# A fused attention and mixture-of-experts kernel: another written-out order for attention, and pass one starting its seven-product form one unit earlier

## The chip, the cores and the metric

One core of a Trainium2 chip runs the whole program in a single launch. The metric is the device time of that launch in microseconds (us). TensorE is called PE here, VectorE DVE, ScalarE ACT, GpSimd POOL, and SP is the queue that issues most DMAs.

## The reference, cut to what matters

```python
# attention: 4 batches x 8 heads, 576 tokens, 64 wide
scores = scale * q @ k.T + (cum[:, None] - cum[None, :])      # cum = cumsum(log f), causal
attn = softmax(scores);  x = (attn @ v) as 2304 tokens x 512
# mixture of experts: 8 experts, 512 -> 1024 -> 512
logits = x @ w_gate;  P = exp(logits - max)
for _ in range(8):                                            # alternate row and column scaling
    P /= P.sum(1) + 1e-9;  P /= P.sum(0) + 1e-9;  P *= N / E
out = sum over e of P[:, e] * (relu(x @ w1[e]) @ w2[e])
```

Everything is fp32. The kernel keeps it so by splitting each operand of a product into a high and a low part (fp32r) and issuing three matmuls: high by high, high by low, low by high.

## The kernel before, in words

**Attention** works on 16 pairs of heads (`attend`, L405). Each pair is cut into some 85 steps, each bound to one engine or to a choice of two. The steps aren't scheduled when the kernel is built: the string `ORDER` lists their numbers, and each engine gets its steps in the order in which they stand there. A letter behind a number picks the engine where a step has a choice (a for ACT, d for DVE, p for POOL). The order also decides which buffer a step gets, since buffers are handed out along the list. The last two steps of a pair write its part of x: the high part (`x_hi_part`, on ACT or DVE) and the low part (`x_lo_part`, L842, on POOL alone). The weight products of the first two blocks of 256 hidden features of expert 0, on the first 768 tokens, are steps too (`early`, lines 904 and 924) and stand between attention's.

**Pass one** takes the remaining 30 blocks (a unit: one expert, 256 of its hidden features) over the same 768 tokens. The loop runs from L1384; unit m computes the hidden features (first half), and the second half of unit m-1 (`second`, line 924: 36 matmuls of 512 columns) follows it. The first half has two forms. `first_plain` (48 matmuls of 384 columns) multiplies x by w1 as they are. `first_fast` (42 matmuls, line 1292) is a seven-product scheme on 2 x 2 blocks. It needs three kinds of prepared operands:

- sums of x: `token_sums` (L1188) forms four sums T1 to T4 for each of two slices c of the contraction, eight additions on POOL each; `part_sums` (L1212) splits them, high on ACT, low by four subtractions on POOL. They are made once for the pass.
- sums of w1: `weight_sums` (L1237) forms S1 to S4, four additions on POOL, for each unit.
- their split: `split_sums` (L1247) rounds on ACT (line 1251 writes all four high sums at once) and subtracts on POOL (line 1255: the four low sums, S1 first; lines 1253 and 1259: low parts of the plain blocks A11, A12, A22). S1 to S4 are kept in the buffer `early_w["w1"]`, which the plain form uses for w1 itself.

```python
    for m, (n, e, fb, segs) in enumerate(work):
        fast, fast_next = m >= PLAIN, m + 1 >= PLAIN
        ...
        if m < KH:
            sums = token_sums(0, m)
            for t in sums:
                pass
```

With `PLAIN = 3` the units 0, 1 and 2 are plain and unit 3 is the first fast one; the sums of x for c = 0 and c = 1 are formed during units 0 and 1. `first_fast` issues its products in the order A11·B11, S2·T2, S1·T1, S3·T3, A12·B21, S4·B22, A22·T4. The tile framework orders pass one by its own estimate, except for instructions pinned by `keep_in_program_order`; what it settles on is fixed when the program is built, and every engine runs its queue in that order. Each fast unit's prepared w1 is also written to DRAM (`keep_w1`). Between the products run the gate's 8 scaling rounds (`gate_weights`, L1133), a few small instructions at each `go_on()`, which the plain form calls four times per unit and `second` six times.

**Passes two and three** (line 1736 and 1838) run the rest of the tokens in the seven-product form on both halves, ordered by a list scheduler (`arrange`). Units whose w1 wasn't kept in pass one are prepared there by `prepare_w1`.

Of the kernel before, what the change touches and what calls it, by code (L numbers as in the profile page):

```python
# [146 lines left out]
def pool_two(n): return 0.02 + n / 410  # L147
# [14 lines left out]
5 4 7 0 9 8 6 10 20 1 3 98 2 21a 95 22d 102 23 17 24 103d 104a 181 11 25a 26d 128 14 93 28 12a 27 349 13a 99 33 94  # L162
15d 29a 34 42 16a 92 30 36 31d 100a 32 56 97 101a 35 43 47 37 44 180 51 57 41 48 61 19 52 58 96 112 45 39 62 445 53
108 40 54 267 113a 63 125 59 114a 269 38 55 126 64 71 183 60 124 110d 75 357 49 73 72a 127 109d 356 50 123 115 116
76a 186 121 79 111 122 81 119a 184 74a 80d 129 139 65 120 182 117d 130 118 185 46 140 82a 83 18 131 141 135 77 187 66
84a 144 268 137 67p 78a 133 85 142 138 149 147 134 68 86a 150 151 69a 70d 199 191 152 148 361 87 200d 202d 153 360
203 201 193d 264 143 145 263 132 204 192d 210 146 194 208 136 195 211 105 89 165 206 88 106 196a 173 159 205 90d 197a
107 166a 169 154 91 171 266 160a 174d 198 167 170a 265 161 163 172a 162d 207 222 1059 164a 168d 1056 212 213 223 227
225 224 209 214 175 226 218 270 216 215 230 219 228 217 1060 220 229 1061 232 1057 234 233 231 246 1058 1062 274 235
189 244 247d 275a 242 188 155p 245a 276d 278 277 243a 190 1068 279d 280a 236 614 289 252 281 615 156 295 221 253d 359  # L170
282 1074 158a 237 362 283a 157a 285d 287 284 256 254 1065 286 290 257a 176 248 534 255a 294 177 296 532 249a 178d 288
291 305 238a 533 301 179 310 297 358 302 306 315 298 444 313 307 293 250 1075 316 292 314 299 363 308 1069 251a 303
317 309 239 318 304 375 311 319 258 448 241d 312 447 240d 446 376d 300 377 378d 379 320 367 272 260 321 332 259 273
368a 383 330 369d 322a 371 271 370 382 331a 336 333d 323 384 372a 340 385 373d 530 1066 328 374 386 342 337a 531 334
387 329d 341a 457 442 388 335d 338 343a 443 458a 625 459d 339a 461 324 460 389 1067 464a 326 261a 626d 344 325 1063
628 380 462d 327 465 381 463 390 262 708 396 528 392 397 394 797 627a 1064 398 393 449 395 403 345 366 391 399 408
365 401 400 1076 346 402 410 406 453 347a 404 350 706 407 348 409 364 455a 454a 547 411 1113 429 550a 1070 618 412
551 351d 469 456 620 1071 405 548d 470 619 549 435 543 467 1072 436d 354 466 425 430a 544d 472 431 352 433 355 474
413 432a 427 617 546 426a 414 494 616 415a 434a 496 471 416 495 421 473 428a 707 497 489 468 1073 529 498 475 535 492
422a 1080 490 493 420 476 1077 491 353 478 480 417 423 477 482 484 418 479 545d 481 419 629 485 424a 539 487 794 486  # L180
633 630d 437 712 541a 631a 488 636d 710 634d 632 483 560 711 635 1078 637 499 793 1079 792 556 521 552 439 509 709
553 522a 517 510a 798 557 511 518a 515 555 512d 451 513 516a 558 507 438 450 514a 554 500 540d 519 452 508a 559 1081
542 501a 520a 502 561 621 575 568 564 570 569 566 580 565 562 578 567 504 1086 571 506 579 1087 573 503 582 563 576
717 505 574 523 581 879 572 1088 878 577 639 583 643 718d 584 642 720 645 440a 656 638 537 524 719a 640 525 593 1110
644 657 536 526a 607 721 641 659 595 658 881 646 1083 594d 722a 796 608d 1084 723a 724 596a 538 441 601 585 713 597
1085 602a 599 598a 603 1082 527 586 600a 647 604a 661 587a 650 588 648 651 605 652 649 664 668 653 666 606d 660 1089
665 667 609 669 654 670 736 589 662 732 591 655 734 663 590 730 731 592 748 671 737 795 689 738 749 624 672 1092 751
750 623 1090 673d 733 690a 687 674 1091 735 685 688a 691 611 799 686a 725 610 683 880 692a 739 612d 622 728a 726a 613
729 684a 753 727 678 740 742 811 746 676 743 1098 744 741 677 1099 754 747 1093 675 1094 814a 756 812a 681 884 889
815 682a 813 882 807 890a 679 820 883 808a 892 693 816 803 680a 817 891d 970 758 809d 821 694a 804d 805a 969 760 755  # L190
823 806 695 1337 819 759 752 967 761 818 757 810 966 824 762 964 965 745 834 822 697 716 696 783 714 835 771 885 784a
763 785 773 786a 775 772a 774d 764 777 776a 837 825 765d 838 698d 766 839 830 778a 699 715 826 700 831 832 968 827
828 840 1336 833 893 829 842 781 1167 841 779 1095 895d 1166 782d 843 846 701d 844 902 767 780a 1100 907 845 836 1101
768 903 979 847 1114 906 769 897 908 983 980d 787 900a 770 909 898a 986a 982 848 704 905 702 981d 901 910 894a 1253
899 987 1111 849 1340 896 1168 1115 850 863 789 788 1170 851a 869 984a 864a 985 1169 861 1112 1102 871 859 870a 790d
# [1891 lines left out]
```

## Time and profile before

| | |
|---|---|
| time, median of 3 runs | 1630.55 us (1630.13 to 1631.98) |
| the profiled execution | 1630.41 us, of which the span of its instructions 1628.6 us |
| PE busy | 1619.9 us, 99% of the span |
| DVE, POOL, ACT busy | 1310.4, 1122.2, 767.3 us |
| attention with the early products | the first 211.6 us |
| pass one | from there to about 690 us |

Matmuls are pipelined: a row of the timeline gives the start of its first matmul and a length up to the modelled end of its last, which overlaps the next row. So the price of a matmul is read from start to start of consecutive rows, or from a count in a stretch, not from the length of one. A bracket at the end of a row is the time its engine idled before it and what ended that.

### The profile page before, as it was taken

How to read it: one execution, taken by the hardware profiler on the slowest of the kernel's cores; microseconds unless marked ns; L12 is line 12 of the kernel's file. 1: busy time of each engine (PE TensorE's matmuls, PEld its weight loads, DVE VectorE, ACT ScalarE, POOL GpSimd, SP SyncE). 2: the span in 40 equal slices, each digit the busy share in tenths (PEclk: the TensorE clock that was granted, in tenths of full speed). 3: DMA queues.
4: the chain of work that ended last, by engine and by line, in shares of the span. 5: the costliest groups of instructions: out<-in, count | busy, mean ns of one | idle time of the engine just before them, and what ended most of it. 6: DMA issues, size and time to landing. Idle time of an engine off the chain costs nothing.

```text
span 1628.6 us, 29751 instructions
## 1 busy us (share of the span) xinstructions
PE 1619.9 (99%) x9641; PEld 1534.1 (94%) x9641; DVE 1310.4 (80%) x2742; ACT 767.3 (47%) x1918; POOL 1122.2 (69%) x1431
## 2 busy tenths in 40 slices
PE   8999999999999999999999999999999999999999
PEld 7888889989899899899999999999999999999998
DVE  8888778776676776788898888878988888788887
ACT  8887743443333333344454444444444444344443
POOL 6556385777788887778777767666666666566675
PEclk9999999999999999999999999999999999999999
DMA  6666325655566656576777776657665555565552
GB/s 154 157 159 160 92 64 175 185 178 185 181 197 184 193 185 209 181 233 192 229 222 220 221 224 201 187 175 218 197 198 162 171 178 170 164 173 171 168 167 70
DMA packets 257025, 291.24 MB, mean 179 GB/s; under 512 B 76291, under 2 KB 168686, under 8 KB 256870
## 3 DMA queue, kind: packets, MB, share of 16 engines
q1 hardware_dynamic: 256438, 288.94, 59.5%
q8 instruction: 77, 1.26, 0.3%
q14 instruction: 78, 0.64, 0.1%
q10 hardware_dynamic: 432, 0.39, 0.1%
HBM read 222.43 MB, written 66.83 MB: 178 GB/s over the span
## 4 chain that ended last, share of the span: by engine, by line
PE 98%; ACT 0%; POOL 0%; DVE 0%; DMA 0%; issue 0%; SPq 0%
PE bankA L1838 28%; PE bankA L1736 20%; PE po L924 16%; PE ph L1292 12%; PE bankM L1736 9%; PE pv L823 3%; PE ph L904 2%; PE pt L775 2%; PE ps L614 2%; PE pq L496 1%; PE ps L660 1%; PE bankA L1889 1%; PE pt L779 0%; PE ps L607 0%; PE bankA L1922 0%; PE pg L858 0%
## 5 line engine op out<-in xcount | busy, mean ns | idle before, releaser
L1847 DVE TENSOR_TENSOR sum<-bankA,sum 128x384 f32<-128x384 f32 x406 | 224.3, 553 | 52.9 <-PE bankA L1838 51.4
L1736 PE MATMUL bankA<-t,wn 128*128 128x384 f32 x1314 | 248.3, 334 | 0.0
L924 PE MATMUL po<-early_w,hh 128*128 128x512 f32 x768 | 239.1, 392 | 0.0
L1736 PEld LDWEIGHTS bankA<-t,wn 128*128 128x128 f32 x1314 | 229.4, 188 | 0.0
L924 PEld LDWEIGHTS po<-early_w,hh 128*128 128x128 f32 x768 | 142.4, 188 | 28.7 <-issue 0.7
L1666 POOL TENSOR_TENSOR fourw<-w 128x256 f32<-128x256 f32 x124 | 91.7, 740 | 92.2 <-DMA w<-in_moe_w_dram 92.2
L924 PE MATMUL po<-early_w,hl 128*128 128x512 f32 x384 | 150.3, 391 | 0.0
L1298 DVE TENSOR_TENSOR u<-ph,u 128x384 f32<-128x384 f32 x189 | 101.9, 552 | 56.8 <-PE ph L1292 53.2
L1337 DVE SCALAR_TENSOR_TENSOR acc<-po,prob,acc 128x512 f32<-128x512 f32 x144 | 106.6, 747 | 50.5 <-PE po L924 48.8
L1838 PE MATMUL bankA<-xhi,early_w 128*128 128x384 f32 x576 | 128.3, 334 | 0.0
L1255 POOL TENSOR_TENSOR early_w<-ws,early_w 128x256 fp32r<-128x256 f32 x108 | 93.9, 898 | 39.7 <-ACT early_w L1251 38.5
L1736 PE MATMUL bankM<-xhi,wn 128*128 128x384 f32 x424 | 119.0, 334 | 0.0
L1232 ACT CAST early_w<-w 128x512 fp32r<-128x512 f32 x66 | 41.0, 622 | 161.1 <-issue 137.9
L1838 PE MATMUL bankA<-xlo,early_w 128*128 128x384 f32 x522 | 116.8, 335 | 0.0
L1529 POOL TENSOR_TENSOR w2n<-fourw,w2n 128x256 fp32r<-128x256 f32 x105 | 79.6, 761 | 43.2 <-PE bankA L1838 21.5
L1838 PE MATMUL bankA<-xhi,w2n 128*128 128x384 f32 x480 | 108.9, 334 | 0.0
L1233 POOL TENSOR_TENSOR early_w<-w,early_w 128x512 fp32r<-128x512 f32 x56 | 71.9, 1305 | 44.8 <-ACT early_w L1232 44.8
L1838 PEld LDWEIGHTS bankA<-xhi,early_w 128*128 128x128 f32 x576 | 102.4, 188 | 0.0
L1838 PE MATMUL bankA<-xlo,w2n 128*128 128x384 f32 x438 | 99.4, 334 | 0.0
L910 ACT ACTIVATE hh<-u 128x384 fp32r<-128x384 f32 x108 | 56.1, 522 | 91.4 <-DVE u L1298 91.3
L1529 POOL TENSOR_TENSOR early_w<-w,early_w 128x256 fp32r<-128x256 f32 x96 | 72.4, 760 | 37.7 <-ACT early_w L1524 37.7
L1529 POOL TENSOR_TENSOR early_w<-fourw,early_w 128x256 fp32r<-128x256 f32 x117 | 89.5, 772 | 12.0 <-ACT early_w L1524 11.3
(332 smaller groups left out, 4518.6 us busy)
## 6 DMA issues: line engine op xcount, KB each, us to landing
wn<-w1d SPq DMA_DIRECT2D x440, 256.0 KB
w<-in_moe_w_dram SPq DMA_DIRECT2D x266, 256.0 KB
w1d<-early_w SPq DMA_DIRECT2D x54, 512.0 KB
w1d<-wa SPq DMA_DIRECT2D x54, 384.0 KB
w1d<-four SPq DMA_DIRECT2D x70, 128.0 KB
dn<-cum_d SPq DMA_DIRECT2D x14, 576.0 KB
pb<-p_d SPq DMA_DIRECT2D x16, 384.0 KB
q<-in_q_dram SPq DMA_DIRECT2D x32, 128.0 KB
```

Source lines behind the costliest of these rows:

```text
L910: nc.scalar.activation(out=hh[:, 0:w], in_=ph[:, 0:w], func=AF.Relu)
L924: nc.tensor.matmul(po[:, cols], ht[:, ts], wt[:, ft, cols], start=(ft == 0 and n == 0), stop=(ft == FB - 1 and n == 2))
L1233: a = lo_on.tensor_tensor(out=lo[:, s], in0=r, in1=hi[:, s].bitcast(F32), op=ALU.subtract)
L1255: nc.gpsimd.tensor_tensor(out=wsum[1][:, n], in0=t[:, n], in1=wsum[0][:, n].bitcast(F32), op=ALU.subtract)
L1292: nc.tensor.matmul(ps, ws[y][:, c], xs[z], start=(c == 0 and m == 0), stop=(c == KH - 1 and m == 2))
L1298: nc.vector.tensor_tensor(out=out, in0=in0, in1=in1, op=ALU.add)
L1337: a = nc.vector.scalar_tensor_tensor(out=to, in0=po, scalar=prob[:, t, e:e + 1], in1=to, op0=ALU.mult, op1=ALU.add)
L1529: eng(e).tensor_tensor(out=dst(1), in0=src(), in1=dst(0).bitcast(F32), op=ALU.subtract)
L1666: eng(en).tensor_tensor(out=vs[o](), in0=a(), in1=b(), op=op)
L1736: nc.tensor.matmul(ps, wt[:, y, c * P:(c + 1) * P], x[z], start=(start and c == 0 and m == 0), stop=(c == KH - 1 and m == 2), skip_group_c ...
L1838: nc.tensor.matmul(at_(b)[:, 0:HT], at_(w)[y][:, k * P:(k + 1) * P], at_(h)[:, z], start=(i == 0), stop=(i == 5))
L1847: nc.vector.tensor_tensor(out=to, in0=at_(b)[:, 0:HT], in1=to, op=ALU.add)
```

## The change

- `ORDER` is replaced throughout. The steps are the same but for the choices of engine: 47 go from ACT to DVE, 46 from DVE to ACT, and the last step of the last pair, its low part of x, goes to DVE.
- `x_lo_part` may run on DVE for the last four pairs (it does for the last one only).
- `PLAIN` is 2: unit 2 is now the first fast unit, and its prepared w1 is kept.
- The sums of x for c = 0 are formed on DVE. Those for c = 1 stay on POOL. All are formed and split in unit 0, c = 1 after c = 0.

```diff
 ORDER = """
-5 4 7 0 9 8 6 10 20 1 3 98 2 21a 95 22d 102 23 17 24 103d 104a 181 11 25a 26d 128 14 93 28 12a 27 349 13a 99 33 94
+0 1 5 4 20 6 7 22a 9 10 2 21a 23 24 25a 26d 102 104a 103d 126 11 12a 33 34 27 8 28 29a 31d 32 30 13a 99 100a 101a 14
...
-        z = step(i + 0.73, {"POOL": pool_two(S)}, x_lo_part, after=[a], uses=[xf])
+        lo_on = {"POOL": pool_two(S), "DVE": dve_sbuf(S)} if i >= NPAIR - NP else {"POOL": pool_two(S)}
+        z = step(i + 0.73, lo_on, x_lo_part, after=[a], uses=[xf])
...
-    def token_sums(g, c):
+    def token_sums(g, c, on=nc.gpsimd):
...
         def pinned(**kw):
-            tc.keep_in_program_order(nc.gpsimd.tensor_tensor(**kw))
+            a = on.tensor_tensor(**kw)
+            if on is nc.gpsimd:
+                tc.keep_in_program_order(a)
...
-    PLAIN = 3
+    PLAIN = 2
...
-        if m < KH:
-            sums = token_sums(0, m)
+        if m == 0:
+            sums = token_sums(0, m, nc.vector)
             for t in sums:
                 pass
...
-        if m < KH:
-            part_sums(0, m, t)
+        if m == 0:
+            part_sums(0, 0, t)
+            for t in token_sums(0, 1):
+                pass
+            part_sums(0, 1, t)
```

The program's matmuls go from 9305 to 9299: 48 of the plain form less, 42 of the fast form more. Line numbers behind L842 are one to six higher in the changed kernel.

Three places show what moved. The first is the start of PE's queue, in attention; `pq` are the turned q and k of the first pair, `pc` the spread decay (from `cumparts`), `ps` the first scores. Before:

```order
L337 MATMUL warm<-ones 128x128 x8
L496 MATMUL pq<-ident,q 128x128 x4
L389 MATMUL pc<-cumparts,pick 128x288 x2
L496 MATMUL pq<-ident,k 128x128 x4
L389 MATMUL pc<-cumparts,pick 128x288 x4
```

And now:

```order
L337 MATMUL warm<-ones 128x128 x8
L496 MATMUL pq<-ident,q 128x128 x4
L496 MATMUL pq<-ident,k 128x128 x4
L389 MATMUL pc<-cumparts,pick 128x288 x4
L537 MATMUL pq<-ident,rz_105 128x128
```

The turning of k stands ahead of the spread of the decay, no longer behind its first half. Over the whole of attention PE changes its kind of work 206 times before and 194 times now, by the same count on both orders.

The second place is POOL's queue from the end of attention to the first fast unit. `early_w_110` is the low part of w1 or of its sums, `ts` the sums of x, `t_4214` and `t_4237` their low parts for c = 0 and c = 1, `ws` the sums of w1, `wa_4236` the low parts of A11, A12 and A22. Before:

```order
L330 TENSOR_TENSOR xlo<-xf,xhi 128x576 x5
L1233 TENSOR_TENSOR early_w_110<-w,early_w_109 128x512 x2
L1197 TENSOR_TENSOR ts<-xhi,xlo 128x384 x2
...
L1197 TENSOR_TENSOR ts<-ts,xlo 128x384
L1220 TENSOR_TENSOR t_4214<-ts,t_4214 128x384 x4
L1197 TENSOR_TENSOR ts<-xhi,xlo 128x384 x2
...
L1197 TENSOR_TENSOR ts<-ts,xlo 128x384
L1220 TENSOR_TENSOR t_4237<-ts,t_4237 128x384 x4
L1241 TENSOR_TENSOR ws<-w 128x256
...
L1255 TENSOR_TENSOR early_w_110<-ws,early_w_109 128x256 x4
```

And now:

```order
L1236 TENSOR_TENSOR early_w_110<-w,early_w_109 128x512 x2
L1223 TENSOR_TENSOR t_4214<-ts,t_4214 128x384 x4
L1198 TENSOR_TENSOR ts<-xhi,xlo 128x384 x2
L1198 TENSOR_TENSOR ts<-ts,xhi 128x384
L1256 TENSOR_TENSOR wa_4236<-w,wa_4235 128x256
...
L1262 TENSOR_TENSOR wa_4236<-w,wa_4235 128x256
L1198 TENSOR_TENSOR ts<-xhi,ts 128x384
L1198 TENSOR_TENSOR ts<-ts,xlo 128x384
L1223 TENSOR_TENSOR t_4237<-ts,t_4237 128x384 x4
L1244 TENSOR_TENSOR ws<-w 128x256
...
L1258 TENSOR_TENSOR early_w_110<-ws,early_w_109 128x256 x4
```

The eight sums for c = 0 are gone from POOL; the rest of the chain keeps its order, with the three low parts of A11, A12 and A22 moved in among the sums for c = 1. In the elided parts stand the other sums, one instruction each.

The third place is PE's queue where the second half of unit 0 ends and the first half of unit 2 begins. Before:

```order
L924 MATMUL po<-early_w_112,hh_4244 128x512
L924 MATMUL po<-early_w_111,hl_4245 128x512
L904 MATMUL ph<-xhi,early_w_109 128x384
L904 MATMUL ph<-xlo,early_w_109 128x384
L904 MATMUL ph<-xhi,early_w_110 128x384
```

And now:

```order
L925 MATMUL po<-early_w_112,hh_4244 128x512
L925 MATMUL po<-early_w_111,hl_4245 128x512
L1295 MATMUL ph<-xhi,wa_4235 128x384
L1295 MATMUL ph<-xlo,wa_4235 128x384
L1295 MATMUL ph<-xhi,wa_4236 128x384
...
L1295 MATMUL ph<-t_4214,early_w_109 128x384 x2
L1295 MATMUL ph<-t_4214,early_w_110 128x384
```

Six matmuls of A11·B11 come first; the next product, S2·T2, reads the high sums of w1 (`early_w_109`) and at its third matmul the low ones (`early_w_110`).

## Rows read from the trace of the kernel before

**Rows 1.** The page, part 1 (busy time and instructions) and part 4 (the chain).

```profile
PE 1619.9 (99%) x9641; PEld 1534.1 (94%) x9641; DVE 1310.4 (80%) x2742; ACT 767.3 (47%) x1918; POOL 1122.2 (69%) x1431
...
PE 98%; ACT 0%; POOL 0%; DVE 0%; DMA 0%; issue 0%; SPq 0%
```

**Rows 2.** Busy us by stretch: PE, PEld, DVE, ACT, POOL, clock, DMA share, GB/s.

```profile
0.00:211.58 211.58, 207.50 (x1812) 168.85 (x1813) 167.39 (x590) 166.66 (x527) 111.06 (x198) 1.00 0.54 139
...
900.00:1000.00 100.00, 100.00 (x579) 100.00 (x578) 87.55 (x178) 48.07 (x123) 72.97 (x95) 1.00 0.72 215
```

**Rows 3.** Who PE waited for: us in total, times, longest.

```profile
PE pc L389 <- DVE cumparts L1032: 1.6, 1, 1.6
```

**Rows 4.** PE's timeline at the start: start, length, engine, line, count.

```profile
1.05 3.62 PE L337 MATMUL warm<-ones 128*128 128x128 f32 x16 [1.05 <-DVE ones L334]
4.66 0.63 PE L496 MATMUL pq<-ident,q 128*128 128x128 f32 x4
```

**Rows 5.** PE's timeline where attention ends and unit 0 begins.

```profile
208.69 0.74 PE L924 MATMUL po<-early_w,hh 128*128 128x512 f32 x2
209.27 0.40 PE L924 MATMUL po<-early_w,hl 128*128 128x512 f32 x1
...
211.75 0.34 PE L904 MATMUL ph<-xlo,early_w 128*128 128x384 f32 x1
212.25 0.61 PE L904 MATMUL ph<-xhi,early_w 128*128 128x384 f32 x2 [0.16 <-POOL early_w L1233]
...
213.24 0.34 PE L904 MATMUL ph<-xlo,early_w 128*128 128x384 f32 x1
213.95 0.62 PE L904 MATMUL ph<-xhi,early_w 128*128 128x384 f32 x2 [0.37 <-POOL early_w L1233]
```

**Rows 6.** PE's timeline: last of unit 0's first half, its second half, unit 2.

```profile
220.82 0.34 PE L904 MATMUL ph<-xhi,early_w 128*128 128x384 f32 x1
...
230.85 0.63 PE L924 MATMUL po<-early_w,hh 128*128 128x512 f32 x2
...
239.32 0.33 PE L904 MATMUL ph<-xhi,early_w 128*128 128x384 f32 x1
```

**Rows 7.** ACT's timeline: first split of x's sums, and the sums of w1.

```profile
221.97 0.82 ACT L1217 CAST t<-ts 128x768 fp32r<-128x768 f32 x1
...
247.96 1.05 ACT L1251 CAST early_w<-ws 128x1024 fp32r<-128x1024 f32 x1 [1.46 <-PE ph L904]
```

**Rows 8.** POOL's timeline from the first split of x's sums to w1's low sums.

```profile
222.89 4.37 POOL L1220 TENSOR_TENSOR t<-ts,t 128x384 fp32r<-128x384 f32 x4
227.34 2.05 POOL L1197 TENSOR_TENSOR ts<-xhi,xlo 128x384 f32<-128x384 f32 x2
...
236.45 4.09 POOL L1220 TENSOR_TENSOR t<-ts,t 128x384 fp32r<-128x384 f32 x4
...
249.09 2.82 POOL L1255 TENSOR_TENSOR early_w<-ws,early_w 128x256 fp32r<-128x256 f32 x4 [2.46 <-ACT early_w L1251]
```

**Rows 9.** Two of POOL's lines over the run: count, ns least, median, most.

```profile
L1197 POOL TENSOR_TENSOR ts<-ts x8: 1008/1020/1481, 218.3 to 598.4; 128x384 f32<-128x384 f32 x8
L1255 POOL TENSOR_TENSOR early_w<-ws,early_w x108: 727/790/1165, 249.1 to 656.9; 128x256 fp32r<-128x256 f32 x108
```

**Rows 10.** DVE's timeline: operands from SBUF, 512 columns, beside a busy and an idle POOL.

```profile
230.53 2.91 DVE L1233 TENSOR_TENSOR early_w<-w,early_w 128x512 fp32r<-128x512 f32 x2 [0.48 <-ACT early_w L1232]
...
256.53 0.69 DVE L1233 TENSOR_TENSOR early_w<-w,early_w 128x512 fp32r<-128x512 f32 x1
```

**Rows 11.** Timelines of PE and of DVE at the gate's last round.

```profile
315.25 0.28 PE L1171 MATMUL pc<-cs,ones 128*128 128x8 f32 x2
317.32 0.60 PE L1182 MATMUL pt<-ident,prob 128*8 128x128 f32 x4
...
313.32 1.04 DVE L913 SCALAR_TENSOR_TENSOR hl<-u,hh 128x384 fp32r<-128x384 f32 x1
316.69 0.31 DVE L1175 TENSOR_TENSOR prob<-prob,ca 128x144 f32<-128x144 f32 x1
```

**Rows 12.** Busy us by stretch, behind PE's last matmul.

```profile
1624.65:1628.50 3.85, 0.00 (x0) 0.00 (x0) 0.48 (x2) 0.16 (x1) 0.00 (x0) 1.00 0.62 204
```

More of the change, by code (lines that the diff above doesn't have):

```diff
@@ L167 @@
[L167 to L171, printed above, removed]
@@ new lines @@
+615 614 61 40 38 49 50 19 112 113a 114a 266 265 183 41 125 45 71 124 59 60 73 127 62 64 75 116 184 185 181 111 79 74a
+115 72a 121 128 81 117d 118 349 139 119a 120 76a 82a 130 186 65 80d 123 140 46 129 144 142 143 122 187 135 66 67p 83
+131 204 84a 77 78a 137 138 133 208 134 147 85 86d 149 150 68 69a 70d 151 152 136 148 191 193d 264 192d 194 263 145
+153 132 199 200a 268 267 202d 203 201 141 87 107 88 106 105 89 90d 210 146 195 359 196a 358 167 168a 173 174a 169
+170a 163 164d 198 206 159 160a 161 162a 197a 207 269 165 166a 171 222 91 1059 1056 213 212 172d 227 225 226 223 224
@@ new lines @@
+205 218 219 154 216 217 175 1060 228 229 211 230 214 215 209 220 270 189 155p 1061 232 233 1057 231 234 235 188 246
+247d 274 275a 356 357 276d 277 242 243a 1058 278 280a 444 445 279d 290 244 245a 236 281 288 1074 252 253d 289 287 221
+237 448 156 157a 282 285d 362 283a 286 361 158a 1068 294 256 257a 284 295 1062 254 255a 177 250 251a 176 238a 178d
+179 190 296 297 298 301 302 360 305 306 307 310 248 249a 315 1065 1075 317 313 314 447 291 316 292 303 304 1069 299
+300 293 308 309 363 385 386 380 384 382 318 388 319 311 312 375 376d 532 378a 377 534 239 241d 258 271 272 273 387
@@ new lines @@
+1091 691 692a 683 684a 677 739 740 675 612a 613 753 676 746 817 747 803 804a 805a 1336 889 891a 890a 965 744 678 807
+808a 809a 881 742 743 754 819 755 818 750 685 821 756 757 823 892 820 741 966 1098 1099 1093 1094 758 760 806 752
+686d 759 761 824 762 880 811 814d 812d 813 815 883 882 884 695 715 714 810 834 697 696 745 763 964 785 786a 835 783
+784a 771 772a 773 774d 775 776a 816 822 837 777 778a 1337 764 838 698d 699 885 908 825 828 902 826 906 830 907 829
+765d 766 827 839 836 831 716 840 909 841 842 843 700 701d 703 705 702 704 770 768 779 780d 781 782a 844 845 1100 1101
@@ new lines @@
+887 886 888 952d 953 954a 875 945 946a 943 944d 1253 947 983 986d 987 984a 985 1340 1341 936 948a 949 950a 937d 938
+997 1004 1005 1006 1011 998 999 1342 1002 1003 1012 1013 996 1171 1193 1191 1188 1189 941 1107 1108 1018 939 1007
+1190 1008 1014 1015 1195 1016 1425 1000 1001 1192 1347 1349a 1251 942 940 959 972 1009 1194 1175 1109 1339 1010 974
+1017 1019 1020 1196 1021 1043 1044d 1419 973 1355 1358a 1356d 1357 1359 1256 1255 1424 1176a 1178 1348a 1350 1123
+1124 1125 1126 961 1119 1022 1023a 1024 1257 1039 1040a 1177a 960 1027 1026 1025 1028 1031 1032d 1117 1118 1029 1030d
@@ new lines @@
+1041 1042a 1254 876a 877 1250 1035 1036d 1033 1034a 1216 1217 1218 1219 1282 1037 1038a 1197 1202 1203 1200 1201 1279
+1278 1198 1199 1274 1204 1205 1275 1127 1206 1207 1209 1208 1276 1210 1280 1211 1214 1281 1215 1212 1213 1277 1128
+1129 1130 1131 1132 1120 1121 1220 1265 1267a 1266d 1268 1422 1421 1351 1353d 1352d 1354 1045 1046 1047 1174 1173
+1172 1269 1270a 1271 1272a 1273 1343 1237 1238a 1261 1263a 1262a 1264 1420 1243 1244d 1229 1230a 1233 1234a 1221 1231
+1232a 1235 1236d 1239 1240a 1241 1242a 1222 1223a 1224 1226 1225 1227 1228 1133 790a 791 1283 1286 1287 1360 1284
@@ new lines @@
+1285 1364 1288 1289 1365 1290 1291 1361 1297 1298 1299 1363 1300 1301 1367 1292 1293 1294 1366 1295 1362 1296 1140
+1141 1142 1302 1303 1134 1135 1304 1434 1435a 1436d 1305 1306 1368 1426 1438 1441d 1442 1439d 1440 1307 1050 1051a
+1054 1053 1052 1055 1378 1379 1445 1380 1381 1382 1449 1437 1245 1246 1260 1259 1308 1309d 1310 1247 1325 1326a 1323
+1324d 1329 1330d 1319 1320a 1315 1316a 1048d 1317 1318d 1430 1432d 1431a 1433 1258 1321 1322a 1327 1328a 962a 963
+1369 1374 1448 1375 1370 1371 1443 1376 1377 1444 1372 1373 1447 1313 1314 1311 1461 1462 1463 1464 1465 1383 1384
@@ L220 @@
+1152 1153 1154 1155 1156 1157 1502 1503d 1507 1506 1504 1505 1158 1159 1160 1161 1162 1163
 """
```

78 lines of the change are left out of this document (26 added, 52 removed).

## The prediction

> **What bounds the kernel now.** I read the page first. PE is busy 99% of the span, and 98% of the chain that ended last runs over PE [rows 1]. So the time is the sum of PE's matmuls, and another engine matters only where PE would have to wait for it. Next I read the busy time by stretch, to see where PE has room: in a stretch of the later passes it runs 579 matmuls of 384 columns in 100 us [rows 2], 0.173 us each, without a gap. An edit can gain there only by taking matmuls out. In attention PE lacks 4.1 of 211.58 us, while DVE and ACT are busy 167 us each [rows 2]: little to win, and two engines near enough to PE to lose by. Last I read the timelines around the end of attention, where the change moves most, because the question there is when the sums that the first fast unit needs are ready.
>
> The sum is made on the profiled execution's 1630.41 us, which lies 0.14 us under the median of 1630.55.
>
> **Unit 2 in the fast form.** 48 matmuls become 42: 6 x 0.173 = **-1.04 us**.
>
> **The low part of x of the last pair, on DVE.** At the start of unit 0 two matmuls come late behind POOL's low part of w1 [rows 5]: from 211.75 to 212.25 and from 213.24 to 213.95 pass 0.50 and 0.71 us, where 0.173 is due, so 0.33 + 0.54 = 0.87 us are lost. POOL makes that low part behind the low parts of x, one of which now leaves its queue. I take both losses as gone: **-0.87 us**; at worst nothing is won.
>
> **The order of attention.** PE changes its kind of work 12 times less, by the two orders. One change costs some 0.1 us: the first two matmuls behind one took 0.58 us from start to start [rows 5], against 0.47 for two of 512 columns at (239.32 - 230.85) / 36 = 0.235 us each [rows 6]. That would be 1.2 us at most, and part of it lies in waits already. At the start k's four transposes, about 0.11 us each, move into the wait of 1.6 us for the decay [rows 3], worth up to 0.4. Against this stands that every step has got a new place in the queues of ACT and DVE, each 79% busy there [rows 2], and a step a microsecond late on them stops PE. I take **-0.8 us**, between -3 (nearly all that PE lacks there) and +2.
>
> **The sums of x and w1 for unit 2: the term that decides.** Before, the first fast unit was unit 3, and POOL had 16 us more. Now PE needs them in unit 2, right behind the second half of unit 0. I keep the times of the trace before; the gains above shift PE and what hangs on it alike. PE begins unit 2 at 239.32 [rows 6]. A11·B11 takes 6 x 0.173, so S2·T2 begins at 240.36, and its third matmul, the first to read the low sums of w1, is due at 240.71.
>
> When do these arrive? By the new order POOL has to do, in one line: the split for c = 0 (4), the sums for c = 1 (8) with three low parts of A11, A12 and A22 among them, the split for c = 1 (4), the sums of w1 (4); then ACT rounds these, and POOL subtracts S1 and S2. The line can't begin before ACT has rounded the sums for c = 0. That cast still stands behind ACT's fourth relu of unit 0, which needs unit 0's last matmul (started at 220.82 [rows 6]); before, it ran at 221.97 for 0.82 us [rows 7], and POOL went on at 222.89 [rows 8]. So taking the sums for c = 0 off POOL does not start this line earlier: POOL idles instead. That DVE has them by then I take for granted: eight additions of 384 columns need 8 x 0.75 x 0.69 = 4.1 us by the row of 512 columns beside an idle POOL, twice that beside a busy one (2.91 for two) [rows 10], and POOL has nothing to do meanwhile.
>
> From 222.89 on, by medians and rows: split 4 x 1.07 = 4.3 (4.37 and 4.09 for four [rows 8]); sums 8 x 1.02 = 8.2 plus 0.3 (227.34 to 236.45 took 9.1 for eight, of which I count a third of the excess, since DVE has less beside it); three low parts 3 x 0.79 = 2.4; split 4.1; sums of w1 4 x 0.79 = 3.2; the cast 1.05 [rows 7] with a hand-over of 0.08 on either side (247.96 + 1.05 to 249.09 [rows 8]), 1.2; S1 and S2, half of 2.82, 1.4 [rows 8, 9]. Sum 25.1: the low sums are there at 248.0, **PE waits 7.3 us**. By the least values (4.1 + 8.1 + 2.2 + 4.1 + 2.9 + 1.2 + 1.4 = 24.0) it waits 6.2, by the most for the short ones (4.4 + 9.1 + 3.5 + 4.4 + 4.7 + 1.2 + 1.5 = 28.8) 11.0. Nothing gives this back, as PE has no gap behind it that it could fill. The rest of the unit's chain holds: S3 and S4 follow 0.7 us apart, and a product takes 1.04.
>
> **The gate.** Unit 2 no longer calls `go_on()` four times, so the last round comes later, in one go. Now two of DVE's low parts (about 0.5 us each; two took 1.04 [rows 11]) stand between the last column sum and the scaled `prob`. Before, from the sum's matmul to the transposes passed 2.07 us [rows 11]; now about 3.0, with ten matmuls of 0.23 between: **+0.6 us**, from 0 to 1.5.
>
> **The clock.** In all rows the granted clock is 1.00, 2.4 GHz, also in the 3.85 us behind PE's last matmul [rows 12]. A wait of 7 us in mid-run has no row. From a rest the trace shows one start: the first 16 records of 128 columns took 3.62 us, 0.22 each, where four transposes of 128 columns right behind took 0.63 with the tail of the last, so 0.11 to 0.16 each [rows 4]. That is half the pace, though the clock stands as granted there too, and at 0.11 a record these 16 lose 1.7 us. I bound the cost by 0 (the idle row) and 3.4 (twice that loss), and take **+1.7**, since the wait is longer than any idle row that kept the clock. The Trainium skill, "TensorE: Matmul & The Clock Gate", in its part on the clock gate, says that the array falls to half its clock when PE has rested, and gets it back only after sustained work. No run here shows it in mid-run; by that rule the 1.7 is due, without it the sum is 1635.6.
>
> **Costed at nothing.** One `prepare_w1` less in the later passes takes work from POOL, ACT and DVE, where PE has no gap [rows 2]. The kept w1 of unit 2 adds four DMAs to SP's queue in a stretch whose loads run ahead of use; if they came late, unit 3's operands would, and PE reaches these only some 8 us after unit 2. The other three late low parts of x stay on POOL. The loads of unit 1's w1 now stand ahead of the gate's stores on SP; PE reads those some 9 us later.
>
> **Sum:** 1630.41 - 1.04 - 0.87 - 0.8 + 7.3 + 0.6 + 1.7 = **1637.3 us**.
>
> **Rivals.**
> - *The clock stays up through the wait.* All else as above, 1635.6. For it: no row falls, even behind the last matmul; against: the start from rest.
> - *POOL is in time, and the kernel isn't slower.* 25 instructions would have to fit in 240.71 - 222.89 - 1.2 = 16.6 us, 0.67 each; from there on there is no wait, and no rest for the clock to fall in. Then 1630.41 - 1.04 - 0.87 - 0.8 + 0.6 = 1628.3. For it: some of POOL's rows are stretched while DVE works beside it; against: the least value of the long ones is 1.01 us, of the short ones 0.73 [rows 9].
> - *Attention's new order makes ACT or DVE late*, some 2.5 us over my term: 1639.8. For it: both are 79% busy; against: the steps are all but the same, and few change engine on balance.
> - *Attention's new order wins 3 us*: 1635.1. For it: 4.1 us that PE lacks; against: 2.7 of these are the start and the wait for the decay.
>
> **How the numbers follow.** A measurement of this kernel can tell 0.2%, 3.3 us, from no change. Chances: the forecast 0.46, the clock kept 0.27, POOL in time 0.12, attention late 0.09, attention winning 0.06. The range leaves out POOL in time and the ends of the others: from 1632.5 (clock kept, the least wait, attention at -2) to 1641.0 (the forecast with 2 us more of wait and clock, attention at +1). Above 1633.8 lie the forecast, the clock kept, attention late and nearly all of attention winning less the low ends: slower 0.83. Within 0.2%: most of POOL in time, and those ends: 0.13. Faster only if POOL is in time and attention wins: 0.04.
>
> **What would show it.** Right: PE idle for 6 to 8 us behind A11·B11 of unit 2, its wait ended by ACT's cast and then by POOL's low sums; POOL idle for some 10 us before its first split, waiting for ACT's cast; matmuls behind the wait 0.32 to 0.35 us apart instead of 0.173 for about 3 us; the two late matmuls at the start of unit 0 gone; 42 matmuls in unit 2. Wrong: no such gap; POOL's additions near 0.7 us; attention's end moved by more than 3 us either way.

## The result, and the profile after

The changed kernel takes 1642.97 us (median of 6 runs, 1640.91 to 1644.18), the kernel before 1630.48 (6 runs beside it, 1629.96 to 1631.98). The ratio is 1.0073, with a 95% interval of 1.0062 to 1.0083: slower, by over three times what can be told from no change. The forecast of 1637.3 had the sign right and the size at about half. The profiled execution took 1642.77 us with a span of 1641.0, so 12.4 us more of span.

The page's parts 1 and 4, beside [rows 1]:

```profile
PE 1624.2 (99%) x9635; PEld 1534.8 (94%) x9635; DVE 1309.6 (80%) x2744; ACT 768.8 (47%) x1919; POOL 1118.8 (68%) x1428
...
PE 78%; DVE 0%; ACT 0%; issue 0%
```

The six matmuls are gone, yet PE is busy 4.3 us longer. Of that 3.1 us lie in attention (210.59 us busy, against 207.50 in [rows 2]), where the clock stayed at 1.00 and the modelled end of a matmul covers a short wait behind it; in pass one some matmuls ran slower. The shares of the chain add up to 78% only, so it was not followed over the whole span and says less than before.

Where the 12.4 us lie follows from the starts of PE's first `ph` and `po` matmuls of each unit in both traces:

| stretch | before | after | difference | forecast |
|---|---|---|---|---|
| attention, to unit 0's first half | 211.58 | 216.27 | **+4.69** | -0.8 |
| units 0 and 1, first halves | 19.27 | 18.20 | -1.07 | -0.87 |
| unit 0, second half | 8.47 | 15.58 | **+7.11** | 0 |
| unit 2, first half | 8.57 | 7.31 | -1.26 | -1.04, then +9.0 for wait and clock |
| the rest (the gate) | | | +2.9 | +0.6 |

**The wait in unit 0.** PE's timeline in the second half of unit 0, from its first matmul to the first of unit 2 (start, length, engine, line, operation, count, and in brackets the idle time before):

```profile
234.47 0.63 PE L925 MATMUL po<-early_w,hh 128*128 128x512 f32 x2
...
238.61 0.40 PE L925 MATMUL po<-early_w,hl 128*128 128x512 f32 x1
243.84 1.22 PE L925 MATMUL po<-early_w,hh 128*128 128x512 f32 x2 [4.83 <-DVE acc L1337]
244.86 0.63 PE L925 MATMUL po<-early_w,hl 128*128 128x512 f32 x1
245.28 1.05 PE L925 MATMUL po<-early_w,hh 128*128 128x512 f32 x2
246.14 0.63 PE L925 MATMUL po<-early_w,hl 128*128 128x512 f32 x1
...
250.05 0.33 PE L1295 MATMUL ph<-xhi,wa 128*128 128x384 f32 x1
```

PE has no free bank until DVE has added an earlier `po` to `acc`. What held DVE is two queues away. POOL, ACT and DVE before that moment:

```profile
226.55 4.19 POOL L1223 TENSOR_TENSOR t<-ts,t 128x384 fp32r<-128x384 f32 x4 [11.19 <-ACT t L1220]
```

```profile
238.19 0.84 ACT L1220 CAST t<-ts 128x768 fp32r<-128x768 f32 x1 [7.18 <-POOL ts L1198]
240.91 0.83 ACT L1220 CAST t<-ts 128x768 fp32r<-128x768 f32 x1 [1.88 <-POOL ts L1198]
241.65 0.86 ACT L911 ACTIVATE hh<-ph 128x384 fp32r<-128x384 f32 x2
247.73 1.05 ACT L1254 CAST early_w<-ws 128x1024 fp32r<-128x1024 f32 x1 [5.22 <-POOL ws L1247]
```

```profile
242.16 1.02 DVE L914 SCALAR_TENSOR_TENSOR hl<-ph,hh 128x384 fp32r<-128x384 f32 x2 [9.23 <-ACT hh L911]
243.10 1.28 DVE L1337 TENSOR_TENSOR acc<-po,acc 128x512 f32<-128x512 f32 x2
```

POOL idles 11.19 us and splits c = 0 only from 226.55. Its sums for c = 1 follow, and ACT's two casts of them wait until 238.19 and 240.91. These stand in ACT's queue ahead of unit 1's last two relus, though PE's last matmul for them started before 234.47. DVE's low parts of those relus wait 9.23 us, and its additions to `acc` behind them. When PE then gets to S2·T2 of unit 2, at 251.12, the low sums of w1 lie ready (ACT's cast ends at 248.78, and POOL subtracts S1 and S2 from 248.86 on in about 0.99 us each): the wait forecast there has nothing left to bite on.

**The clock.** Behind each stretch and its length stand the busy us of PE, PEld, DVE, ACT and POOL, the granted clock, the DMA share and GB/s, for single microseconds:

```profile
240.00:241.00 1.00, 0.00 (x0) 0.00 (x0) 0.00 (x0) 0.09 (x1) 1.00 (x2) 1.00 0.95 323
242.00:243.00 1.00, 0.00 (x0) 0.00 (x0) 0.84 (x2) 0.51 (x2) 1.00 (x2) 0.50 0.00 0
249.00:250.00 1.00, 1.00 (x6) 0.83 (x5) 0.86 (x2) 0.43 (x1) 1.00 (x2) 1.00 0.77 239
```

The granted clock falls from 1.00 (2.4 GHz) to 0.50 (1.2 GHz) during the wait and is back at 1.00 in the microsecond from 249. In between matmuls of 512 columns start 0.427 us apart (244.86 to 246.14 above for three), where [rows 6] have 0.235. That makes some 2.1 of the 7.11 us, the wait 5.0.

**Attention.** What PE computes between the `pv` (the products with v) of two consecutive pairs is nearly the same in both orders, within four matmuls. Three stretches take over 1 us longer: pair 8 to 9, 11.69 before and 12.99 after; 9 to 10, 10.87 and 11.94; 11 to 12, 14.84 and 16.96. They make 4.49 of the 4.69 us; the others differ by up to 0.6 either way and cancel. Here is the longest of them, before and then after, in the columns of the table of clocks above:

```profile
159.81:174.65 14.84, 14.84 (x146) 12.12 (x145) 13.43 (x44) 11.57 (x40) 7.24 (x18) 1.00 0.58 156
```

```profile
162.28:179.23 16.95, 15.58 (x145) 11.94 (x144) 11.79 (x40) 12.02 (x39) 10.36 (x20) 1.00 0.53 149
```

The plainest chain, pair 13's preparation, lies in the last stretch; here ACT, DVE and PE:

```profile
162.25 0.58 ACT L911 ACTIVATE hh<-ph 128x512 fp32r<-128x512 f32 x1
162.73 0.61 ACT L317 CAST early_w<-w 128x512 fp32r<-128x512 f32 x1
163.24 0.78 ACT L678 ACTIVATE er<-er,mn 128x576 f32<-128x576 f32 x1
164.01 0.25 ACT L317 COPY qr<-pq 128x128 f32<-128x128 f32 x1
168.12 0.28 ACT L319 ACTIVATE qz<-pq 128x128 fp32r<-128x128 f32 x1 [2.30 <-DVE kT L485]
```

```profile
164.29 0.69 DVE L322 CAST kT<-pq 128x512 fp32r<-128x512 f32 x1 [3.01 <-ACT qr L317]
```

```profile
165.81 0.63 PE L496 MATMUL pq<-ident,q 128*128 128x128 f32 x4
167.38 0.27 PE L781 MATMUL pt<-ident,er 128*64 128x128 f32 x1 [0.94 <-DVE kT L485]
```

DVE's `kT` reads the bank `pq` that ACT's small copy `qr` reads as well. The kernel never lets two engines read one bank at once; which of them goes first is settled by the list. In the new list `qr` is first, ACT has three longer steps ahead of it, and DVE stands still for 3.01 us; then ACT waits 2.30 for DVE, and PE for both. Before, `kT` stood first and waited for PE's own product only:

```profile
159.48 0.69 DVE L322 CAST kT<-pq 128x512 fp32r<-128x512 f32 x1 [1.26 <-PE pq L496]
```

The Trainium skill, "PSUM — Partial Sum Buffer", in its section on bank collisions, says that two engines on one bank at once, readers included, are an error and have to be kept apart by waits. The rows agree with the waits; that they could be left out no run here shows. The preparation of pairs 11 and 12 has the same with q and k, the first of it in the stretch from 9 to 10: the high part of k on ACT stands behind the rest of q on DVE.

```profile
137.24 0.21 ACT L317 CAST kT<-pq 128x64 fp32r<-128x64 f32 x1 [2.09 <-DVE qz L481]
```

In the stretch from 8 to 9 the rows show something else, a broadcast by DMA that DVE's `xf` waits for; no run tests it. The stretch differs from profile to profile (11.95 to 12.99 with the new order, 11.69 to 11.92 with the old).

```profile
127.93 0.49 DVE L832 TENSOR_TENSOR xf<-pv,rb 128x320 f32<-128x320 f32 x1 [1.71 <-DMA rb<-r]
```

**The gate.** Between 338 and 364 us PE loses four times, as it waits for the gate's small steps, which come in one go now. PE's waits by what ended them (us in total, times, longest):

```profile
PE po L925 <- DVE acc L1340: 1.0, 1, 1.0
PE pt L1183 <- DVE prob L1176: 0.7, 1, 0.7
PE pt L1183 <- ACT ps L1185: 0.4, 1, 0.4
```

From start to start these places are 0.84, 0.6, 1.2 and 0.2 us longer: 2.8 of the 2.9.

### The profile page after: what moved, and what is told of

Read it like the earlier page. It is cut to its first block, busy times and chain, and to the rows that moved or that the text cites. A ratio compares the mean times of both kernels' runs of the same rounds, so it can differ in the third digit from the quotient of the medians.

```text
span 1641.0 us, 29744 instructions
## 1 busy us (share of the span) xinstructions
PE 1624.2 (99%) x9635; PEld 1534.8 (94%) x9635; DVE 1309.6 (80%) x2744; ACT 768.8 (47%) x1919; POOL 1118.8 (68%) x1428
## 3 DMA queue, kind: packets, MB, share of 16 engines
q8 instruction: 77, 1.26, 0.3%
## 4 chain that ended last, share of the span: by engine, by line
PE 78%; DVE 0%; ACT 0%; issue 0%
PE bankA L1844 28%; PE bankA L1742 20%; PE po L925 11%; PE ph L1295 9%; PE bankM L1742 9%; PE bankA L1895 1%; PE bankA L1928 0%; PE bankM L1895 0%; DVE hl L914 0%; PE bankM L1928 0%; DVE acc L1340 0%; DVE tn L322 0%; DVE u L322 0%; ACT u L317 0%
## 5 line engine op out<-in xcount | busy, mean ns | idle before, releaser
L1301 DVE TENSOR_TENSOR u<-ph,u 128x384 f32<-128x384 f32 x196 | 105.7, 552 | 59.1 <-PE ph L1295 57.0
L1258 POOL TENSOR_TENSOR early_w<-ws,early_w 128x256 fp32r<-128x256 f32 x112 | 98.6, 910 | 34.0 <-ACT early_w L1254 30.6
```

What stands on the lines that cost most here:

```text
L1258: nc.gpsimd.tensor_tensor(out=wsum[1][:, n], in0=t[:, n], in1=wsum[0][:, n].bitcast(F32), op=ALU.subtract)
L1301: nc.vector.tensor_tensor(out=out, in0=in0, in1=in1, op=ALU.add)
```

## The experiments

The theory after the result: two separate faults (bank readers out of turn in attention; casts ahead of relus in pass one), the gate third, and a real gain of about 2 us under them. "Before" is always the run beside it, within 0.6 us of 1630.5. A time without a ratio is a single run.

**The halves apart.** Edits: the kernel before with the new `ORDER` and `x_lo_part` alone; the changed kernel with the old `ORDER` and old `x_lo_part`; the kernel before with only the last pair's low part of x on DVE.

```diff
 # e3, in the ORDER of before
-... 1501 ...
+... 1501d ...
```

> Edit: the kernel before with the new ORDER and the low part of x of the last pair on DVE; pass one as before (PLAIN = 3, all sums of x on POOL, c = 1 in unit 1). Theory (the new order itself costs the attention part, whatever follows): unit 0's first half ends 3.6 us later than before (224.4 instead of 220.82), the two late matmuls at unit 0's start are gone, and the span is 1628.6 + 3.6 = 1632.2, within 0.5. Rival (attention's loss hangs on pass one, for example through the loads of its weights, which stand in the same queue): unit 0's first half ends at about 220, span about 1627.7.

> Edit: the changed kernel with the order of before and the low part of x of the last pair on POOL again; PLAIN = 2 and the sums in unit 0 as in the change. Theory (the two parts add up): attention as before, the two late matmuls at unit 0's start still there, then PE waits some 5 us in the second half of unit 0 for DVE's accumulation, and the gate costs some 2 to 3 us; span 1628.6 + 12.4 - 3.6 = 1637.4, within 1. Rival (pass one's loss comes from attention ending late, or is shared with it): span below 1634.

> Edit: the kernel before with one step moved: the low part of x of the last pair on DVE instead of POOL, at the same place in the order. Theory: the two late matmuls at the start of unit 0 go, 0.87 us, all else stays: span 1627.7, within 0.2. Rival: DVE's other work there is pushed back and PE waits for it instead; span 1628.4 or more.

The order alone: 1633.17, ratio 1.0014 (1.0004 to 1.0023), span 1630.8. Unit 0 starts at 214.87, 3.3 late: 9 to 10 and 11 to 12 are as long as in the changed kernel, and 8 to 9 takes 11.95. Pass one alone: 1639.79, 1.0055 (1.0040 to 1.0070), span 1637.6. So 2.2 and 9.0 us of span, 11.2 of the 12.4; most of the rest is the stretch from 8 to 9. The low part alone: 1631.07, ratio 1.0000 (0.9991 to 1.0009), no gain: the two late matmuls of [rows 5] are gone, but PE loses 0.93 us at 213.34, waiting for DVE. Here is that row of PE's timeline:

```profile
214.45 0.44 PE L905 MATMUL ph<-xhi,early_w 128*128 128x384 f32 x1 [0.71 <-DVE acc L935]
```

There DVE's low part of w1 ahead of that addition took 1.70 us beside a busy POOL, against 0.69 in the changed kernel, where POOL is idle. With the new order the first halves of units 0 and 1 do get shorter, by 0.82 us in the run with the order alone and by 1.07 in the changed kernel. No run has the new order without this edit, so which of the two wins them is not shown. (The new order also moves one step that the section on the change doesn't list, 1477, a copy at the end of attention, from DVE to POOL.)

**Attention's waits mended.** The kernel of the order alone, with three swaps in the list. In pairs 11 and 12 the two steps that write the high parts from a bank now go ahead of the two that write the low parts; in pair 13 both parts of `kT` go ahead of `qr`.

```diff
-1186a 1187 1184a 1185
+1184a 1186a 1185 1187
-986d 987 984a 985
+984a 986d 985 987
-1265 1267a 1266d 1268
+1265 1266d 1268 1267a
```

> Edit: the kernel of the run with the new order alone (PLAIN = 3), with three local swaps in the order and nothing else: in pairs 11 and 12 the high part of k's last rows goes ahead of q's on the bank that both are read from, and in pair 13 DVE's two parts of k go ahead of ACT's copy out of the same bank. Theory (the new order loses where two engines read one bank in turn, each step waiting for the one ahead of it in the list, and that one stands behind other work on its own engine): PE's extra time between the products of pairs 9 and 10 falls by 1.0 us, between those of pairs 11 and 12 by 2.1 us; span 1630.8 - 3.1 = 1627.7, within 0.5 (1.3 more where the late broadcast of the norms in pair 8 turns up again). Rival (ACT and DVE are simply late there, whatever the order on the banks): the waits move on to the next step, span 1630.0 or more.

1630.11 against 1630.78, ratio 0.9996 (0.9987 to 1.0005), span 1628.3. Pair 11 to 12 fell from 17.00 to 14.94 (14.84 before), and 9 to 10 from 11.93 to 11.65; in later runs with the swaps the latter took 10.88 to 11.28. So the list's order at these places is the cause from 11 to 12, shown by moving a handful of steps, and of most of the loss from 9 to 10, where the runs scatter. What the new order wins beyond that is nothing: unit 0 starts at 212.39 here, and at 211.79 to 212.26 in the later runs, against 211.58 before.

**Where the wait in unit 0 comes from.** First, c = 1 summed on DVE in the same buffer; then the kernel before with the sums alone moved (`PLAIN` 3, old order).

```diff
 # e4
-            for t in token_sums(0, 1):
+            for t in token_sums(0, 1, nc.vector):
```

> Edit: the changed kernel with the sums of x for c = 1 on DVE too, which sits idle from 232.4 to 242. POOL loses eight additions, 8.1 us. Theory (the wait hangs on POOL's line of sums, through ACT's cast that stands ahead of unit 1's last relus): ACT's casts for c = 1 run at about 234 and 236 instead of 238.2 and 240.9, DVE's accumulation is not held, the 5 us wait and the half-clock stretch go, S2's low sums are there by about 242 before PE needs them; unit 2 wins its 1.04; span 1641.0 - 5 - 2.3 - (0 to 1) = 1633.2 to 1634.2. Rival (DVE becomes the engine that is late, since its queue also holds the relus' low parts and the accumulation): PE still waits 2 us or more for DVE, span above 1636.

> Edit: the kernel before with one part of pass one's change: the sums of x for c = 0 on DVE and those for c = 1 formed and split in unit 0, with PLAIN = 3 as before, so that unit 2 needs none of them. Theory (the 5 us wait comes from where the split of c = 1 stands in ACT's queue, ahead of unit 1's relus, not from unit 2's need): PE still waits for DVE's accumulation in the second half of unit 0, 2 to 3.5 us, since only the three low parts of w1 (2.2 us) leave POOL's line ahead of it; span 1631 to 1633. Rival (the wait is tied to the fast unit 2): no wait there, span 1628.6 within 0.5.

The first came out at 1640.46, ratio 1.0055 (1.0040 to 1.0070), worse than expected. DVE's second sums need the buffer `ts`, which POOL's split still reads, and DVE stands for it with the gate behind. DVE's row, and PE's wait for the gate:

```profile
230.72 2.09 DVE L1198 TENSOR_TENSOR ts<-xhi,xlo 128x384 f32<-128x384 f32 x2 [1.36 <-POOL t L1223]
```

```profile
PE pc L1172 <- DVE cs L1167: 2.4, 1, 2.4
```

Unit 2 runs in 7.30 us without a wait, but PE reaches it 4.3 us late, so this doesn't show that the sums were early enough. The second (1636.94) has no fast unit 2, and PE waits all the same:

```profile
PE po L924 <- DVE acc L1336: 5.2, 1, 5.2
```

So the wait comes from the place of the split in ACT's queue, not from the earlier fast unit.

**The split behind the relus.** The edit makes c = 1's split an item of unit 1, with the casts for w1 pinned behind it and so behind the relus.

```diff
 # e8
-            part_sums(0, 1, t)
+        if m == 1:
+            part_sums(0, 1, t)
```

> Edit: the changed kernel with the split of the sums for c = 1 put behind unit 1's relus, and ACT's casts for the sums of w1 pinned behind them too; POOL still makes the sums for c = 1. Theory (with the relus free, the prediction's own wait comes to light, since POOL's line ends no earlier): no wait for DVE in the second half of unit 0, but PE waits 4 to 6 us in the first products of unit 2, for POOL's low parts, and the clock falls behind it; span 1639 to 1641. Rival (the relus' wait was all): no wait in unit 2, span 1633 to 1634.

1647.45. Unit 0's second half is back at 8.47, so the split's place ahead of the relus was the cause there. A wait in unit 2 appears instead, for POOL's low parts of w1:

```profile
PE ph L1296 <- POOL wa L1257: 5.7, 1, 5.7
```

It stands one product earlier than forecast, inside A11·B11, since the pins put the low part of A11 behind POOL's line as well. PE's row, and POOL's low sums:

```profile
250.12 1.01 PE L1296 MATMUL ph<-xhi,wa 128*128 128x384 f32 x2 [5.70 <-POOL wa L1257]
```

```profile
250.03 2.79 POOL L1259 TENSOR_TENSOR early_w<-ws,early_w 128x256 fp32r<-128x256 f32 x4
```

The second of these four, S2's, is ready at about 251.4; PE began unit 2 at 243.92, so without the wait for A11 it would have been due at about 245.3. By this estimate the forecast wait would have been some 6 us. In the changed kernel the other wait came first and covered it. Half clock follows (to 254.95), and 2.8 us more go in unit 1's second half, in waits for DVE. The place ahead of the relus is thus not the dearer one: this kernel is slower than the changed one.

**Sums early on DVE, own tiles; then the gate.** The first edit gives c = 1 tiles of its own (u0 to u3) and pins the cast of w1's sums for unit 2 behind unit 1's relus; the second also restores the four `go_on()` in unit 2.

```diff
 # e6
-            for t in token_sums(0, 1):
+            for t in token_sums(0, 1, nc.vector, True):
...
-                split_sums(r1, ws)
+                split_sums(r1, ws, m == 1)
 # e7, besides, in first_fast's product()
+            if b in ("T1", "B21", "B22", "T4")[:calls]:
+                go_on()
```

> Edit: the changed kernel with the sums of x for c = 1 on DVE as well, but in four tiles of their own (those that hold the products later), so that they need not wait for POOL's split of c = 0, and ACT's casts for the sums of w1 pinned behind unit 1's relus. Theory (unit 2's fast form pays as soon as nothing waits in a queue ahead of unit 1's relus): DVE has the sums by about 230, POOL splits both in one go from 226.5 to 235, the sums of w1 are split by 242 and PE needs them at 244.8; no wait and no half clock in the second half of unit 0; the gate's flush stays (2.9 us); span 1641.0 - 5.0 - 2.3 - 0.4 = 1633.3, or 1.3 less where attention doesn't meet its late broadcast. Rival (the wait moves to DVE's accumulation or to S2): PE waits 2 us or more between 235 and 250, span above 1635.

> Edit: the kernel of the run with the early sums, plus the four calls that drive the gate on, put back into unit 2 behind four of its products. Theory (the gate's 2.9 us come from its last steps being run off in one go because four calls are missing): the waits at 338, 346 and 360 us go, span 1633.3 - 2.9 = 1630.4, or 1.3 less where attention doesn't meet its late broadcast. Rival (those waits belong to the gate's last round wherever it falls): span within 1 us of the run without the calls.

1641.23, 1.0063 (1.0046 to 1.0080), and 1638.63, 1.0047 (1.0032 to 1.0062). The second half of unit 0 takes 8.47 in the first, and the gate's 2.9 us are gone in the second, as expected. But a new wait stands one unit later, of the same make. ACT of the second:

```profile
250.03 0.40 ACT L1264 CAST wa<-w 128x256 fp32r<-128x256 f32 x1 [6.78 <-DMA w<-in_moe_w_dram]
```

```profile
250.87 0.69 PE L1306 MATMUL ph<-xhi,wa 128*128 128x384 f32 x1 [3.86 <-ACT u L1318]
```

The cast of unit 3's w1 waits for its load and stands ahead of the copy of unit 2's first product, which PE needs; half clock follows to 255.

**All mends together, on the new order and on the old.** The copy goes ahead of unit 3's cast (`issue_after`), and the three swaps are in (e9) or the old order (e10).

> Edit: the kernel of the run with the early sums and the gate's calls, with the three swaps in attention's order, and ACT's first cast for the next unit's w1 set behind the copy of unit 2's first product. Theory (each wait found so far was a step that stood in a queue ahead of one PE needed; with all of them moved, the change pays what its matmul count says): no wait of PE over 1 us behind attention; unit 0 starts at about 212.4, unit 2's first half takes 7.3 us, clock 1.00 throughout; span 1628.3 (mended order, PLAIN = 3) - 1.3 = 1627.0, 1.6 below the kernel before, within 0.5. Rival (another queue is late next, for example POOL's sums for unit 3, since w1 for unit 3 lands only at about 250): PE waits 1 us or more in unit 3 or 4, span 1628 or more.

> Edit: the same pass one, with the order of before and the low part of x of the last pair on POOL again. Theory: attention as before, the two late matmuls at unit 0's start stay (0.87 us), pass one wins 1.3: span 1628.6 - 1.3 = 1627.3, within 0.5. Rival (pass one's gain needs what the new order does at the end of attention, a POOL that is free early): PE waits in unit 2 for POOL's low sums, span 1628.5 or more.

1633.27, 1.0017 (1.0008 to 1.0025), and 1632.98, 1.0016 (1.0007 to 1.0025). No wait over 1.5 us is left, but DVE, with eight more additions, comes late in several places; two of them in e9:

```profile
PE ph L905 <- DVE early_w L1246: 1.3, 1, 1.3
...
PE po L925 <- DVE acc L1348: 0.8, 1, 0.8
```

**Shared between the engines.** Three more arrangements with own tiles, pinned casts, swaps and gate: c = 1 summed on POOL in its idle time (e12); then unit 1's low parts of w1 ahead of DVE's last sums, and c = 1 split first (e13); all sums on DVE, unit 1's low parts on POOL (e14).

```diff
 # e12
+            for t1 in token_sums(0, 1, own=True):
+                pass
 # e13, besides
+            with tc.issue_after(low.ins):
+                for t in sums:
+                    pass
 # e14
-                split_whole("w1", r1, nc.vector)
+                split_whole("w1", r1, nc.gpsimd)
```

> Edit: the kernel of the run with everything mended, but the sums of x for c = 1 go back to POOL, in tiles of their own and into the 10 us in which POOL idles ahead of its first split, and the gate's last four rounds are spaced by four calls instead of five, in place of the calls inside unit 2. Theory (DVE's eight extra additions and the gate's steps inside unit 2 were what made DVE late in the run with everything mended: 1.45 us in unit 1, 2.4 us behind units 2 and 3): unit 0 starts at about 212.4, unit 1's first half and the second halves behind the fast units take what they do in the kernel before (no row of PE waiting for DVE over 0.5 us up to 280); unit 2 wins its 1.3 us; span 1628.3 - 1.3 = 1627.0, within 0.5, less than the kernel before in the profile though no more than 0.1%. Rival (the fast form in unit 2 costs DVE more than it has, wherever the sums are made): PE waits 1.5 us or more for DVE's accumulation behind units 2 and 3, span 1628.3 or more.

> Edit: the kernel of the run with the sums on both engines, with one more step of order: DVE makes the two low parts of unit 1's w1 ahead of its last four sums of x instead of behind them, and the split of c = 1 (whose sums POOL has first) goes ahead of that of c = 0. Theory (the only wait left in that run, 3.6 us in unit 1 and the half clock behind it, 3.1 us, comes from where DVE's queue holds those two low parts, behind additions that take 0.9 to 1.4 us beside a busy POOL instead of 0.55): no wait in units 0 to 3 over 0.5 us, clock 1.00 throughout, span 1633.6 - 6.6 = 1627.0, within 0.6, which is 1.6 below the kernel before. Rival (the two engines slow each other so far that something else PE needs is late next, in unit 1 or at S2): PE waits 1 us or more before 260 us, span 1628.6 or more.

> Edit: the early sums again, all sixteen of x on DVE, but unit 1's low parts of w1 go from DVE to POOL, which idles there, and ACT's casts for the sums of w1 are pinned behind the relus of unit 2 as well as of unit 1; the gate's last rounds spaced by four calls, attention's order mended. Theory (each wait so far was a cast that stood in ACT's queue ahead of relus while it waited for POOL, or an engine given more than its turn): DVE and POOL no longer add at the same time except for some 3 us, no cast stands ahead of a relu in units 1 and 2; PE waits at most 0.6 us before 280 us, span 1627.0 to 1627.8. Rival (with a fast unit 2 the load of unit 3's w1, which can start only when POOL has done with unit 2's, makes unit 3 late): PE waits 1 us or more in unit 3 for POOL's low sums, span 1628.6 or more.

1636.24, 1.0036 (1.0022 to 1.0049); 1637.73, 1.0044 (1.0030 to 1.0058); 1633.22, 1.0016 (1.0007 to 1.0025). In e12 one wait over 1 us is left, behind additions that both engines make at once and more slowly; half clock follows it:

```profile
PE ph L905 <- DVE early_w L1246: 3.4, 1, 3.4
```

An addition on DVE, in the changed kernel with POOL idle, and then in e12 beside POOL:

```profile
221.40 0.55 DVE L1198 TENSOR_TENSOR ts<-ts 128x384 f32<-128x384 f32 x1
```

```profile
218.83 1.38 DVE L1201 TENSOR_TENSOR ts<-ts 128x384 f32<-128x384 f32 x1
```

In e13 that wait is gone and three others come: 1.25 us in unit 2, 2.4 in unit 1's second half behind ACT's cast of unit 3's sums, and half clock. In e14 the first half of unit 2 and the second half of unit 1 run without a wait (7.31 and 8.57); 1.24 us go in unit 1, 0.92 in the second half of unit 2 and 1.2 in the gate. None of these beats the kernel before; the mended order alone is the same as it. Whether some arrangement keeps unit 2's gain stays open.

## Why the prediction was right or wrong

- **Unit 2 in the fast form, -1.04:** right. The first half took 1.26 us less, in the changed kernel as in e12 and e14, where PE waited neither in it nor in unit 0's second half (7.31). Some 0.2 of that is no gain: two small matmuls of the gate stood in this half before and stand elsewhere now.
- **The low part of x, -0.87:** the loss is gone in the changed kernel (-1.07), but the step named as the reason gave nothing alone, as a wait for DVE took its place. So the number came right without its mechanism being shown.
- **The order of attention, "I take -0.8 us": the step that failed.** It measured +4.7, outside even its own bounds of -3 to +2; the 5.5 us between are nearly all of the 5.7 by which the forecast fell short; the other errors (the gate +2.3, the sums and the clock -1.9, the two small gains -0.4) cancel by luck. The step priced changes of PE's kind of work and gave "every step has got a new place in the queues of ACT and DVE" a bound of 2 us without reading those queues. The runs showed in its place: pairs of steps on two engines that read one bank wait on each other in the list's order, and three such places out of turn cost 2 to 3 us between them, which three swaps give back; a late broadcast costs up to 1.3 more in some executions. Fewer changes of kind were worth nothing that shows. The rival "attention late" named the right engines, with 2.5 us over the term where 5.5 came.
- **The sums for unit 2, 7.3 us of wait:** the size nearly right, the place and the engine between wrong. POOL idled 11.19 us before its first split, as the step worked out, so its line ran late; but the first to suffer was ACT's queue, where casts of those sums stand ahead of relus, 5.0 us in unit 0. Then PE was late enough for the rest. The step followed POOL's line to its reader on PE, and left out what stands behind the waiting cast on ACT. That 5.0 came so near to 7.3 is in part luck, since PE waited for the relus and not for S2's low sums. That a wait of the forecast's size stood behind it, the run with the split behind the relus makes likely (5.7 us in unit 2, though for the low part of A11).
- **The clock, +1.7:** right (about 2.1), with half the pace in working matmuls behind the wait. The rival without it is out. The start from rest was a sound guide: in the changed kernel's trace the transposes of q, from 4.62 us on, start 0.213 us apart, and the last ones of k, from 5.78 on, 0.11. The trace's own record of the granted clock begins there, at 5.78 us (at 4.38 in the kernel before), so the 1.00 printed for the time ahead of it is no reading.
- **The gate, +0.6:** too small; +2.9, and the run with four calls in unit 2 gives it back. The step priced one late round; four places in the gate's last rounds came late. It also took the 1.04 us in [rows 11] for two low parts; the row is one (x1).
- **Costed at nothing:** right. Passes two and three are unchanged (938.3 us before and 937.9 now, from the first to the last matmul), and no load came late in the changed kernel.
- **The range:** its low end is said to add up from the kept clock, the least wait and attention at -2; that sum is 1633.3, not 1632.5. The measured time lies above the high end, 1641.0, by the error on attention.

By the measured terms: 4.7 - 1.1 + 7.1 - 1.3 + 2.9 = 12.3, the difference of 12.4 but for rounding.

## What to carry to other kernels

Before costing a new order, read for each engine what stands behind every instruction that waits: a cast that waits for a slow engine, put ahead of a relu whose data is there, stopped PE for 5.0 us before the cast's own reader was due. Where two engines read one bank, the order of the list is a wait; put the reader first whose engine is free first, and look at those pairs before counting anything else. And where a queue is that full, mending one wait shows the next, so test the mended sum before counting on the gain beneath it.

## What the runs showed of the hardware that was not expected

The granted clock and the waits don't go together simply. With pass one alone, the same wait on the second half of unit 0 (4.83 us in the row) keeps 1.00 throughout, and the clock falls only after PE has resumed. PE's row, and the microseconds behind it:

```profile
240.83 0.88 PE L924 MATMUL po<-early_w,hh 128*128 128x512 f32 x2 [4.83 <-DVE acc L1336]
```

```profile
240.00:241.00 1.00, 0.17 (x1) 0.17 (x2) 1.00 (x3) 0.00 (x0) 1.00 (x2) 1.00 0.00 0
242.00:243.00 1.00, 1.00 (x4) 0.81 (x3) 0.96 (x2) 0.00 (x0) 1.00 (x2) 0.50 0.00 0
245.00:246.00 1.00, 1.00 (x6) 0.78 (x5) 0.97 (x4) 0.79 (x1) 0.14 (x1) 1.00 0.80 265
```

In the kernel with both sums on DVE in one buffer it fell behind a wait of 2.6 us, with the sums early in own tiles not behind one of 2.7, and the gate's waits of up to 1.2 us never lowered it. The Trainium skill, "TensorE: Matmul & The Clock Gate", in its part on the clock gate, says that the window the hardware looks at runs freely, so that the same rest can fall differently into it; the two kernels with the same wait and a different fall agree with that, and no run here shows more.

The other surprise is how much DVE and POOL slow each other when both add from SBUF: 0.55 us became 0.9 to 1.4 on DVE, and 1.0 became 1.2 to 1.35 on POOL.
